# A residual block on one Trainium2 core: eight VectorE adds of the input transform given to accumulating transfers, with new engine orders

## The chip, the cores and the metric

The kernel runs on one core of one Trainium2 chip. The metric is the device time of one execution in microseconds, lower is better. A core has TensorE (PE: matmuls; PEld is its weight load), VectorE (DVE), ScalarE (ACT), GpSimd (POOL), the DMA-issuing SyncE (SP) and 16 DMA engines. In the profile, L642 is line 642 of the kernel.

## The reference

One residual block of a diffusion network. The input x is 2 images of 512 channels and 64 x 64 pixels, in bf16.

```python
def gn(z, gamma, beta): ...          # group norm over 4 groups of 128 channels, eps 1e-5
def conv3(z, w): ...                 # 3 x 3 convolution, 512 to 512 channels, padding 1
h = conv3(silu(gn(x, g1, be1)), w1)
h = h + (silu(t_emb) @ w_emb).reshape(B, C, 1, 1)
h = conv3(silu(gn(h, g2, be2)), w2)
return x + h
```

## The kernel before

**Tiling.** Layer 0 is the first convolution, layer 1 the second. Each goes over 4 chunks: 2 images (b) of 2 halves (ch) with 32 rows each; chunk n is 2 * b + ch, so the third and fourth chunk are the second image. A chunk has 4 groups, one for each tile of 128 output channels (ot); each group sums over 4 tiles of 128 input channels (ct). Each convolution is done in a transformed form: along the rows of the image four output rows come from six transformed input rows (pos 0 to 5), and for some positions a smaller transform is nested along the columns. So every chunk needs a transformed input V, every output tile a transformed weight U, and each group's results are put together again behind the matmuls.

**What each engine does.** TensorE runs direct matmuls of 512 columns (L935, into `acc` and `mid`) and nested ones of 256 columns (L943, into `nst`). PSUM holds three double banks (`ps_two`: `nst`, `mid` and small helpers) and two single ones (`ps_acc`). In layer 0 the first two groups are flat (no nesting), the third and fourth chunk nest four positions.

- `produce_V` makes V for one chunk, in steps for each ct. `activate` loads the rows into one of two buffers `ak`, and applies normalization and SiLU on ScalarE (L628) into the padded part of the buffer (65 columns a row). `transform` then makes `diff = -4 * same + below` in two instructions, a scaled copy of 128x2080 and an add on VectorE (L642); `diff` lies where the loaded rows lay. Then come an in-place subtraction of rows of the padded part (L649), a scaled copy of 520 elements, and the additions that write V (L669 reads `diff`, L679 reads `diff` and the rows), and `columns` for the nested planes (L559, L564).
- `prep_U` makes U for a weight tile: four scaled copies (1536 or 768 elements), adds on VectorE (L422) and in part an accumulating transfer issued on GpSimd (L433); `nest_U` adds the nested matrices (L395).
- Behind the matmuls of a group: evacuation of PSUM into `rm` (1024 elements) by `evac_nested` or `evac_mid`, column additions on VectorE (L988, L989, L990), row additions and three scaled copies of 512 (L1002 to L1009), evacuation of two single banks into `ring` (`close_group`), then an accumulating transfer z onto y issued on GpSimd (L1070), the store, and sums for the second norm on ScalarE (L796).

**Scaled copies and FLIP.** Every scaled copy and evacuation goes through one helper. `times` has VectorE as its default, `evac` ScalarE; a string of 406 digits, taken one by one in program order, flips the engine where it has a 1. On ScalarE such a copy shows as L308 ACTIVATE, on VectorE as L309 TENSOR_SCALAR.

**Order.** A planner (`_Background`) spreads the work of `produce_V`, `prep_U` and `nest_U` over the groups in program order. At the end `in_order` overrides this: the table `ORDER` gives for each engine the sequence of its instructions by their number in program order, written out by hand as ranges, and each instruction is made to follow the one before it. So each engine's queue is exactly its table.

The lines in which VectorE's first sum stands:

```python
D_BY_DMA = lambda layer, n, ct: False
...
if D_BY_DMA(layer, 2 * b + ch, ct):                 # in activate
    times(diff, same, -4.0)
    nc.gpsimd.dma_start(out=diff, in_=below, accum_op=ALU.add, max_dma_last_dim=CR * WP)
...
if not D_BY_DMA(layer, 2 * b + ch, ct):             # in transform
    times(diff, same, -4.0)
    nc.vector.tensor_tensor(out=diff, in0=diff, in1=below, op=ALU.add)
```

CR * WP is 32 * 65 = 2080 and HW // 2 is 2048.

Of the kernel before, what the change touches and what calls it, by code (L numbers as in the profile page):

```python
# [10 lines left out]
ALU = mybir.AluOpType  # L11
# [53 lines left out]
0-31 90-122 32-43 123 44-56 124 156 125 157-162 126 163-172 127-136 173-181 137-153 182-187 154-155 57-73 188 74-79  # L65
189-252 80-89 254 286 255 287-317 256-258 253 320-335 259-277 336-351 278-285 318 358 370-385 359-360 352-353
386-401 354-355 319 356-357 364-369 408-410 420-423 402-403 424-435 361-362 414 404-407 415-419 363 411-413 458 461
436-451 459 452-453 460 462-463 454 464-465 455 466 470-485 467 456-457 468-469 486-501 511-512 508 502-503 509
514-519 504-507 510 513 520-525 544-549 526-533 550 534-536 551 537 552-553 538-542 592-593 543 554-559 568 560-565
580 566-567 569-570 581-583 571-572 594 573-575 595 576 584-585 596-600 586-589 601-608 624-625 590-591 626-634 609  # L70
635-638 577-579 639-644 610-621 645 648 622-623 646-647 649-654 673 661 674 655-659 675 660 662-670 689 705-716 671
717-721 672 722-725 676 726-728 677-678 690-701 737 702-703 738 704 679-680 749-750 681-687 751-752 688 753-760
739-744 729-730 745 761 731-736 762 746 763 777 747-748 778-779 793-815 780-786 825-826 787-789 816 827 790-792 837
828 764-776 829-835 838 836 839-848 817 849 865 850-851 818 852 819-822 866-867 853-857 823 868-869 824 870-871 858
872 859 873 860-864 874-879 881 880 882-903 905-907 904 913 908 914-915 925 909 916 926 910-912 937-938 917 927-928
939-940 918 929-931 919 953 941-945 954 920 932 946 921 947-949 922 955-957 950 969 923 951-952 924 958 933-936
959-966 970-974 967-968 975 1001 976-978 1002-1004 1013 979-992 1005 1014-1015 993 1006 1016-1018 994 1025-1026
1019-1022 1027 1023 1028-1030 1007 1024 1031-1032 995-1000 1033-1036 1008-1009 1037-1038 1010-1011 1039-1040 1012
1041 1057-1058 1042 1059-1060 1043 1061 1044-1048 1062-1063 1049-1050 1064-1065 1051-1054 1066-1075 1055-1056
1076-1087 1109 1088 1097 1089 1110-1111 1090-1091 1112-1120 1125-1132 1092-1093 1141 1133 1142 1134-1136 1094 1137  # L80
1095 1138-1140 1098-1099 1121-1124 1100 1096 1101-1108 1143-1147 1157-1172 1148-1156 1173-1181 1185-1193 1182-1183
1194 1184 1195-1209 1213 1210-1212 1214-1242 1245-1260 1243 1261-1262 1285-1291 1263-1264 1244 1265-1267 1301-1302
1268-1284 1303-1315 1317-1319 1292 1316 1320-1327 1293-1295 1328-1332 1296-1300 1349-1353 1361-1362 1354-1357
1333-1348 1363 1358-1359 1373-1381 1360 1364 1382-1386 1365-1367 1387-1389 1405 1390-1394 1368-1371 1395-1404 1372
1406-1429 1437 1430-1431 1438-1441 1432-1436 1442-1443 1450-1451 1444-1448 1452-1459 1462-1463 1460-1461 1464
1478-1493 1449 1494-1495 1465-1477 1496-1502 1526-1528 1538 1529-1531 1539-1541 1510-1518 1542 1503-1509 1543
1519-1525 1532-1537 1544-1551 1566-1581 1552-1565 1582-1614 1626-1627 1615-1619 1628-1631 1638-1639 1620-1624 1632
1625 1633-1636 1654-1661 1637 1662-1670 1640-1653 1671-1701 1726-1730 1702 1731 1703 1732-1737 1704-1705 1714-1716
1706-1710 1717-1719 1711-1713 1720-1725 1742-1744 1738-1741 1745-1746 1758 1747-1749 1759-1760 1750-1757 1761-1770
1774-1777 1790-1798 1778-1785 1799 1802 1814 1771 1786-1787 1772-1773 1800 1803-1804 1788-1789 1805 1815-1816  # L90
1806-1809 1801 1810-1813 1830 1846 1831 1847 1832 1848-1853 1833 1854-1861 1834-1835 1862-1864 1817-1829 1865-1869
1836-1845 1894-1909 1870-1874 1882 1910-1912 1883-1891 1913 1926-1928 1875-1881 1929-1930 1914-1918 1892 1931-1940
1893 1919 1941-1951 1920-1925 1952-1961 1974-1985 1962-1963 1990-1992 1964 1993 1965-1967 2006-2007 1968-1969 2008
1994 2009-2012 1995-2000 1970-1971 2001-2005 2013-2015 1972-1973 2016-2025 2030-2033 2026-2028 2034-2035 1986 2036
2042-2045 2037 2046 2029 2047 1987 2048 1988-1989 2049 2038-2039 2050-2053 2040-2041 2054 2070-2071 2086 2055-2056
2087-2088 2057-2059 2089 2060-2064 2090 2072 2091 2065-2069 2073-2075 2092 2076-2077 2093 2078-2085 2094-2101 2110
2102 2111-2113 2103-2105 2123 2114 2124-2131 2115 2106-2109 2116-2117 2135-2136 2132 2137-2140 2151 2141-2145 2133
2118 2146 2167 2152 2119 2147-2149 2153 2120 2150 2134 2154-2156 2121-2122 2157-2159 2168-2171 2160-2164 2172
2165-2166 2173-2178 2183-2198 2179-2181 2199 2182 2200-2201 2211 2202-2205 2212 2223 2206-2208 2224-2226 2239-2241
2227-2231 2255-2258 2232 2259 2213 2260-2263 2242-2243 2214-2217 2209-2210 2218-2219 2244 2220-2222 2245 2233-2236  # L100
2246 2237-2238 2247-2252 2264 2253-2254 2265-2270 2287-2289 2271-2286 2290-2294 2299-2300 2311-2321 2327 2322
2328-2339 2301 2323-2326 2340-2342 2302-2303 2343-2344 2304 2295 2345 2296-2298 2305-2307 2346 2308-2310 2347-2354
2359-2372 2355-2356 2373 2357-2358 2374 2399-2414 2375-2377 2387-2396 2378-2380 2415-2421 2381-2382 2422-2423
2383-2384 2424-2426 2385-2386 2427-2430 2397-2398 2431-2446 2463-2464 2447-2462 2465-2471 2475 2487 2476 2488-2489
2477-2481 2503-2504 2482-2486 2505 2519-2521 2472-2474 2506-2509 2522-2525 2490-2502 2526 2510-2516 2527-2528
2517-2518 2529-2534 2551-2556 2535-2550 2557-2563 2575-2583 2591 2584 2564-2566 2607 2585-2587 2592 2588-2590 2608
2593 2567 2594 2568-2574 2609-2611 2595-2606 2612-2620 2623-2625 2639 2626-2628 2621-2622 2629 2640-2641 2663
2630-2631 2664-2665 2632-2635 2651 2636-2638 2666-2667 2652 2642 2668 2643-2644 2669 2653-2654 2670 2645-2646
2671-2672 2647-2648 2673-2677 2655 2678-2679 2656-2659 2680 2660 2681 2695 2682 2661 2683-2685 2662 2686-2690
2696-2701 2691-2694 2702-2704 2649-2650 2705-2726 2751-2764 2727-2728 2739 2765-2766 2740 2729-2733 2741-2742  # L110
2734-2737 2743 2767-2769 2744 2738 2770-2772 2783-2784 2773-2777 2745 2778 2746 2779-2780 2747-2748 2785-2786
# [76 lines left out]
def kernel(  # L188
# [13 lines left out]
    nc = tc.nc  # L202
# [5 lines left out]
    HW = H * W  # L208
    WP = W + 1
# [5 lines left out]
    CR = TH * TR  # L215
# [7 lines left out]
    D_BY_DMA = lambda layer, n, ct: False  # L223
# [372 lines left out]
    def produce_V(layer, b, ch, resident=None, V=None):  # L596
# [13 lines left out]
        def activate(ct):  # L610
            at, same, below, diff = views(ct)
# [616 lines left out]
```

## Time and profile before

| | |
|---|---|
| time, median of 3 runs | 460.19 us (459.31 to 460.53) |
| the profiled execution | 459.56 us, of which the span from the first to the last instruction is 457.5 us |
| TensorE busy | 444.0 us (97%) |
| VectorE busy | 431.4 us (94%) |
| ScalarE busy | 386.8 us (85%) |
| GpSimd busy | 75.6 us (17%) |
| mean granted TensorE clock | 0.995 |

Busy is the share of time in which an engine has an instruction in it; neighbouring instructions can overlap a little, and a busy TensorE is not TensorE at its peak. A line of a group reads: line, engine, operation, output<-input, shapes, count | busy us, mean ns of one | idle us before them, and who ended it. In the table of waits a line reads: engine, its output, line <- releasing engine, output, line: us in total, times, longest. In the table by stage each line is a stretch: length, then busy us and instructions of PE, PEld, DVE, ACT and POOL, the granted clock, the DMA engines' share and GB/s. In a timeline a line reads: start us, us from the first start to the last end, engine, line, operation, count [idle before <- releaser].

### The profile page before, as it was taken

The numbers are of one execution on the slowest core, as the hardware profiler recorded it, in microseconds if no ns is written. First come the engines' busy times: TensorE is split into PE (matmuls) and PEld (weight loads), VectorE is DVE, ScalarE is ACT, GpSimd is POOL, SyncE is SP. The second block draws the span as 40 slices with busy tenths as digits, with TensorE's granted clock in tenths as the row PEclk, the third lists the DMA queues.
The fourth block names the chain that finished last, engine by engine and source line by source line (L and its number), as shares of the span: only waits on it lengthen the run. The fifth ranks groups of instructions, "written<-read, shape, count | busy, mean of one in ns | idle before, by whom it ended". The sixth has DMA issues, their size and how long they took to land.

```text
span 457.5 us, 8442 instructions
## 1 busy us (share of the span) xinstructions
PE 444.0 (97%) x3238; PEld 288.3 (63%) x3238; DVE 431.4 (94%) x828; ACT 386.8 (85%) x423; POOL 75.6 (17%) x119
## 2 busy tenths in 40 slices
PE   8989999999999999997999999999999999999996
PEld 7944454556555667665556655557666666668874
DVE  2999999999999999999999999998999989999796
ACT  5899999979998798789999999647878697969761
POOL 1222301020000001210121211113221221222110
PEclk9999999999999999999899999999999999999999
DMA  8999765543846462447879895466957768637654
GB/s 311 353 388 243 153 169 150 161 128 104 192 128 159 101 179 64 122 141 210 221 171 262 219 208 117 115 139 163 214 142 185 181 162 210 138 92 150 128 159 165
DMA packets 25011, 80.05 MB, mean 175 GB/s; under 512 B 2827, under 2 KB 6027, under 8 KB 24587
## 3 DMA queue, kind: packets, MB, share of 16 engines
q0 software_dynamic: 10080, 34.87, 37.4%
q1 hardware_dynamic: 14832, 44.64, 28.8%
q8 instruction: 25, 0.41, 0.3%
q14 instruction: 15, 0.12, 0.1%
q10 hardware_dynamic: 59, 0.01, 0.0%
HBM read 42.54 MB, written 16.78 MB: 130 GB/s over the span
## 4 chain that ended last, share of the span: by engine, by line
PE 66%; DVE 18%; ACT 6%; issue 5%; DMA 2%; POOL 1%; SPq 0%; DVEq 0%; ACTq 0%; POOLq 0%
PE nst L943 26%; PE acc L935 23%; PE mid L935 13%; DVE V L679 2%; DVE ak L642 2%; DMA xbuf<-in_x_dram 2%; PE acc L1038 2%; DVE V L559 1%; ACT ak L628 1%; ACT rm L308 1%; ACT ring L796 1%; PE half L935 1%; DVE ak L649 1%; DVE V L564 1%; DVE V L669 1%
## 5 line engine op out<-in xcount | busy, mean ns | idle before, releaser
L943 PE MATMUL nst<-V,U 128*128 128x256 f16 x1600 | 209.5, 272 | 3.6 <-DVE rm L309 2.4
L943 PEld LDWEIGHTS <-U 128*128 128x128 f16 x1600 | 153.8, 97 | 54.8 <-issue 4.7
L935 PE MATMUL acc<-V,R 128*128 128x512 f16 x696 | 182.7, 385 | 2.0 <-DVE V L669 0.9
L935 PEld LDWEIGHTS <-R 128*128 128x128 bf16 x744 | 71.7, 97 | 64.9 <-issue 3.3
L308 ACT ACTIVATE rm<-nst 128x1024 f16<-128x1024 f32 x98 | 97.7, 1023 | 10.2 <-PE nst L943 4.7
L935 PE MATMUL mid<-V,U 128*128 128x512 f16 x336 | 85.1, 384 | 0.7 <-DVE U L422 0.7
L796 ACT ACTIVATE ring<-ring 128x2048 f16<-128x2048 f16 x32 | 61.3, 1914 | 1.6 <-ACT ak L628 0.6
L628 ACT ACTIVATE ak<-ak,nb_all,sc_all 128x2112 f16<-128x2112 f16 (+1 forms) x28 | 60.1, 2153 | 2.3 <-DVE nb_all L527 2.3
L935 PEld LDWEIGHTS <-U 128*128 128x128 f16 x336 | 32.4, 97 | 36.1 <-DVE U L422 1.4
L308 ACT ACTIVATE ring<-ring 128x512 f16<-128x512 f16 x58 | 34.9, 626 | 22.7 <-DVE ring L1002 15.9
L1070 POOL DMA_DIRECT2D ring<-ring x28 | 26.5, 946 | 143.3 <-ACT ring L308 122.1
L308 ACT ACTIVATE ak<-ak 128x520 f16<-128x520 f16 (+1 forms) x34 | 38.2, 1141 | 3.0 <-DVE ak L649 2.8
L642 DVE TENSOR_TENSOR ak<-ak 128x2080 f16<-128x2080 f16 x32 | 39.9, 1248 | 0.1
L679 DVE TENSOR_TENSOR V<-ak 128x1040 f16<-128x1040 f16 x54 | 39.2, 726 | 0.7 <-ACT ak L308 0.5
L990 DVE TENSOR_TENSOR rm<-tu,rm 128x1024 f16<-128x1024 f16 x50 | 34.8, 695 | 1.0 <-ACT rm L308 0.8
L564 DVE TENSOR_TENSOR V<-V 128x512 f16<-128x512 f16 (+1 forms) x62 | 35.3, 577 | 0.0
L559 DVE TENSOR_TENSOR V<-V 128x1024 f16<-128x1024 f16 (+1 forms) x31 | 30.8, 995 | 0.7 <-PE acc L935 0.7
L308 ACT ACTIVATE ring<-acc 128x512 f16<-128x512 f32 x52 | 29.6, 596 | 1.8 <-DVE ring L309 0.8
L422 DVE TENSOR_TENSOR U<-U,g1t 128x1536 f16<-128x1536 f16 x32 | 30.9, 972 | 0.0
L989 DVE TENSOR_TENSOR tu<-rm 128x512 f16<-128x512 f16 x50 | 21.4, 428 | 2.7 <-ACT rm L308 2.5
L649 DVE TENSOR_TENSOR ak<-ak 128x1040 f16<-128x1040 f16 x32 | 23.0, 718 | 0.1
L669 DVE TENSOR_TENSOR V<-ak 128x1040 f16<-128x1040 f16 x32 | 22.9, 715 | 0.0
(132 smaller groups left out, 452.4 us busy)
## 6 DMA issues: line engine op xcount, KB each, us to landing
ring<-ring POOLq DMA_DIRECT2D x28, 512.0 KB, 4.6
ak<-h_scr SPq DMA_DIRECT2D x16, 528.0 KB, 3.9
h_scr<-ring SPq DMA_DIRECT2D x16, 512.0 KB, 3.7
ring<-in_x_dram POOLq DMA_DIRECT2D x14, 512.0 KB, 5.6
out_dram<-ring POOLq DMA_DIRECT2D x14, 512.0 KB, 4.7
ak<-in_x_dram SPq DMA_DIRECT2D x12, 528.0 KB, 4.3
R<-in_w_dram SPq DMA_DIRECT2D x16, 384.0 KB, 4.7
U<-U POOLq DMA_DIRECT2D x14, 384.0 KB, 5.7
```

The source lines that it names most:

```text
L308: return nc.scalar.activation(out=o, in_=i, func=ACT.Copy, scale=f)
L422: nc.vector.tensor_tensor(out=o, in0=i0, in1=i1, op=op)
L559: nc.vector.tensor_tensor(out=lo2.rearrange("p c q (t w) -> p (q t) c w", w=HALF), in0=plane_pair(0, HALF + 2), in1=plane_pair(1, HALF), o ...
L564: nc.vector.tensor_tensor(out=hi2[:, c].rearrange("p q (t w) -> p (q t) w", w=HALF), in0=i0, in1=i1, op=op)
L628: nc.scalar.activation(out=at[:, lo - r0:hi - r0, 1:W + 1], in_=sap, func=ACT.Silu, bias=nb_all[:, layer, b, ct:ct + 1], scale=sc_all[:, l ...
L642: nc.vector.tensor_tensor(out=diff, in0=diff, in1=below, op=ALU.add)
L649: nc.vector.tensor_tensor(out=rows(1, 2), in0=rows(1, 2), in1=rows(3, 2), op=ALU.subtract)
L679: nc.vector.tensor_tensor(out=o, in0=in0, in1=in1, op=op)
L796: behind(nc.scalar.activation(out=junk, in_=y, func=func, scale=scale, accum_out=acc), inst)
L935: nc.tensor.matmul(out, lhsT=w_direct(pos, ct, kx), rhs=rhs, start=first, stop=last)
L943: nc.tensor.matmul(accs["nst", (pos - 1) // 2][bank][:, q, :, plane, :], lhsT=lhsT, rhs=rhs.rearrange("p (t w) -> p t w", w=HALF), start=s ...
L990: nc.vector.tensor_tensor(out=msl[:, 1 - k:4 - k:2].rearrange("p q t w -> p q (t w)"), in0=tu[:].rearrange("p q t e w -> p q (t e w)"), in ...
```

## The change

In the third and fourth chunk of layer 0 (8 cases: 2 chunks, 4 ct) the first sum of the input transform is made in `activate`: the scaled copy, then a transfer issued on GpSimd that adds 2048 of the 2080 elements of each partition (4096 bytes), and an add of the last 32 elements on VectorE. The switch string is another (103 ones instead of 138, of 406), and so are the tables: VectorE has 855 entries instead of 824, ScalarE 354 instead of 385, GpSimd 123 instead of 115; TensorE (3231) and SyncE (103) have as many as before, in another order.

```diff
     "DVE": """
-0 4 3 2 1 14 13 5 7 6 48 8 16 9 15 10 17 11 20 12 19 18 25-26 22 27 21 28 23 29 24 30-31 46 32-33 47 49 34 52 35 53
+0 4 3 2 1 13-14 5 7 48 6 8-10 15-16 11 17 19 18 25 24 12 21 26 20 27 22 28 23 29-32 45 33 38 46 49 47 34 50 35 51 70
...
-    D_BY_DMA = lambda layer, n, ct: False
+    D_BY_DMA = lambda layer, n, ct: layer == 0 and n >= 2
...
-    FLIP = "0100100011000000000000100010010100000110100001110111001100001100110000000011000000010011100000111001000001010000011000100011100000000000100111000010001000000000100000001010100010100000010001000000111011110000000001001101101000000000001110010000100101110011000011011111000001010000000111100000100111010000001111100000001100000100111110000001111100001100111000000111110000001110000110000111000000001010000111"
+    FLIP = "1000110010101011000000000000000010001011100000000111001100000001101100000000000000001100000000000001010000110000000100000001000000000000000000000000110000001000000000000000000000000100000001000000111011100000000000100100010100001001011001010000111000011011000010011101000001000000000001100001000111111000000110000000010000000100111010000001100100000100111000000101110000001100000100000101000000001110000111"
...
             if D_BY_DMA(layer, 2 * b + ch, ct):
                 times(diff, same, -4.0)
-                nc.gpsimd.dma_start(out=diff, in_=below, accum_op=ALU.add, max_dma_last_dim=CR * WP)
+                nc.gpsimd.dma_start(out=diff[:, 0:HW // 2], in_=below[:, 0:HW // 2], accum_op=ALU.add,
+                                    max_dma_last_dim=HW // 2)
+                nc.vector.tensor_tensor(out=diff[:, HW // 2:], in0=diff[:, HW // 2:], in1=below[:, HW // 2:], op=ALU.add)
```

In program order the calls of the string that concern the first chunk of layer 0 are 8, 10, 12 and 14 for the four scaled copies of 2080 elements, and 9, 11, 13 and 15 for those of 520.

The start of TensorE's table, before and after. Entries 352 to 369, 402 to 419, 452 to 469 and 502 to 519 are the first group's matmuls for ct 0 to 3, entries 520 to 591 the second group's; 320 to 351, 370 to 401, 420 to 451 and 470 to 501 are column sums of the second image:

```diff
-... 411-413 458 461 436-451 459 452-453 460 462-463 454 464-465 455 466 470-485 467 456-457 468-469 486-501 511-512 508 502-503 509 514-519 504-507 510 513 520-525 544-549 526-533 ...
+... 414-419 436-451 461-462 458-460 470-485 463 452-454 464-465 455 466-467 456-457 468-469 511 508 512 486-501 509-510 520-528 513 502-505 514 506-507 515-517 529-531 518-519 532-542 ...
```

More of the change, by code (lines that the diff above doesn't have):

```diff
@@ L70 @@
[L70 to L84, printed above, removed]
@@ new lines @@
+1351 1373-1378 1352 1379-1385 1361-1362 1386-1388 1353-1354 1363 1355-1360 1389 1364-1366 1390-1404 1367-1372
+1405-1414 1421-1428 1437 1429-1436 1438-1439 1415 1440 1416-1420 1441-1443 1450-1452 1444 1453-1454 1445 1455
+1446-1449 1456-1464 1478 1465-1470 1479-1484 1471-1476 1485-1486 1477 1526 1494 1487-1491 1495 1492-1493 1496-1507
+1527 1508-1523 1538 1528-1529 1524-1525 1530-1532 1539-1546 1533-1535 1550 1566-1569 1551-1555 1570-1571 1582
+1572-1576 1583 1547-1549 1584 1536-1537 1577 1585-1595 1578-1581 1596-1597 1556-1565 1614-1620 1626 1598-1613
@@ L171 @@
+85 79 89-100 102 101""",
 }
```

181 lines of the change are left out of this document (95 added, 86 removed).

## The prediction

> **What bounds the kernel now.** First the page: busy shares and the granted clock by slice.
>
> ```profile
> PE 444.0 (97%) x3238; PEld 288.3 (63%) x3238; DVE 431.4 (94%) x828; ACT 386.8 (85%) x423; POOL 75.6 (17%) x119
> ...
> PEclk9999999999999999999899999999999999999999
> ```
>
> TensorE is the bound and its matmuls are not touched, so the change can win only where TensorE now waits or is slowed. Next, who TensorE waited for (total us, times, longest):
>
> ```profile
> PE nst L943 <- DVE rm L309: 2.4, 1, 2.4
> ...
> PE nst L943 <- ACT rm L308: 1.2, 3, 0.8
> PE acc L935 <- DVE V L669: 0.9, 1, 0.9
> PE acc L935 <- DVE V L662: 0.8, 1, 0.8
> ...
> PE mid L935 <- DVE U L422: 0.7, 1, 0.7
> ```
>
> Two of these lie in the start (0.9 at 33 us, 0.7 at 46 us). The larger ones lie in the last chunk of layer 0. The table by stage (us; busy of PE, PEld, DVE, ACT, POOL; clock; DMA) shows it:
>
> ```profile
> 150.00:200.00 50.00, 50.00 (x360) 34.38 (x358) 48.67 (x101) 41.24 (x46) 6.52 (x8) 1.00 0.46 128
> 200.00:210.00 10.00, 9.16 (x60) 5.54 (x58) 9.97 (x20) 10.00 (x12) 1.22 (x3) 1.00 0.57 135
> 210.00:220.00 10.00, 7.63 (x58) 5.93 (x57) 10.00 (x20) 9.49 (x14) 1.96 (x3) 0.88 0.66 206
> 220.00:232.00 12.00, 11.18 (x75) 7.09 (x73) 12.00 (x22) 11.38 (x12) 0.81 (x2) 0.96 0.93 238
> 232.00:300.00 68.00, 68.00 (x413) 39.70 (x412) 67.69 (x124) 63.52 (x72) 12.65 (x18) 1.00 0.75 175
> ```
>
> From 200 to 232 us VectorE and ScalarE are both full and TensorE is idle for 0.84 + 2.37 + 0.82 = 4.0 us. From 150 to 207 us the chain that ended last runs through VectorE almost alone. After the 2.37 us the clock is down as well. The timeline shows twelve `acc` matmuls at 2.82 us before and 3.58 us behind it:
>
> ```profile
> 206.30 2.82 PE L935 MATMUL acc<-V,R 128*128 128x512 f16 x12
> ...
> 215.47 1.23 DVE L309 TENSOR_SCALAR rm<-nst 128x1024 f16<-128x1024 f32 x1
> ...
> 219.39 3.58 PE L935 MATMUL acc<-V,R 128*128 128x512 f16 x12
> ```
>
> The granted clock gives the price: 10 x 0.12 + 12 x 0.04 = 1.7 us. With some 0.7 us of shorter gaps the last chunk of layer 0 loses 4.0 + 1.7 + 0.7 = 6.4 us. That is what can be won. The Trainium skill (TensorE: Matmul & The Clock Gate, Part 1) puts the drop to half clock behind an idle window of about 3.4 us. By that rule 2.37 us would cost no clock and 4.7 us could be won; the trace shows the drop, and I take 6.4.
>
> **The eight adds.** In chunks three and four of layer 0 the full add (L642, 128x2080) leaves VectorE; these eight ran at 102.7 to 179.8 us, all ahead of the loss.
>
> ```profile
> L642 DVE TENSOR_TENSOR ak<-ak 128x2080 f16<-128x2080 f16 x32 | 39.9, 1248 | 0.1
> L308 ACT ACTIVATE ak<-ak 128x2080 f16<-128x2080 f16 x13 | 25.3, 1943 | 0.2
> L309 DVE TENSOR_SCALAR ak<-ak 128x2080 f16<-128x2080 f16 x19 | 13.4, 705 | 1.2 <-ACT ak L628 1.2
> L1070 POOL DMA_DIRECT2D ring<-ring x28 | 26.5, 946 | 143.3 <-ACT ring L308 122.1
> ```
>
> Removed: 8 x 1.248 = 10.0 us. Added: eight 32-column tails. No row has that shape. Adds of 512, 1040 and 2080 columns take 428, 718 and 1248 ns, about 0.53 ns a column and 167 ns fixed, so 0.18 us; the 4- and 8-column adds (160 to 200 ns) agree. Eight are 1.4 us. Bounds 0.07 us (the V memset) and 0.43 us (512 columns). VectorE: -8.6 us.
>
> **The switch string.** Ones fall from 138 to 103 of 406, and the tables go from 824 to 855 entries on VectorE and from 385 to 354 on ScalarE: 31 scaled copies net move to VectorE. Walking the string along the calls (the eight -4.0 copies are now called one step earlier) gives, net: 18 row copies of 512 (0.303 us on VectorE, 0.626 on ScalarE), 8 of 520 (0.307, 0.645), 6 weight copies of 1536 (0.565, 1.487), one 2080, one row copy, minus one 768; two evacuations of 1024 go the other way (1.227, 1.023). VectorE: 5.5 + 2.5 + 3.4 + 0.7 + 0.3 - 0.4 - 2.5 = +9.5 us. ScalarE: -25.0 us. So VectorE as a whole stays where it was (-8.6 + 9.5 = +0.9), and ScalarE is relieved. One of the two evacuations is the 1.23 us row at 215.47 that ended the longest wait.
>
> **The transfers.** GpSimd gets 8 more issues (about 0.9 us each, 7 us of an engine at 17%). The DMA engines are 46 to 53% busy at 100 to 200 us, and the nearest transfer (`ring<-ring`, 512 KB, same accumulate) lands 4.6 us after its issue starts, 4.0 to 7.5 over all accumulates. Who waits is the subtraction at L649 or L669 on VectorE, and behind it VectorE's whole queue. In the new table 5.55 to 10.5 us of VectorE rows stand between each copy and the first such reader. Row durations add to 503 us against 431.4 busy, since neighbours overlap, so the cover lasts 0.857 of that: 4.8, 4.9 and 5.1 us for the three tightest (third, first and fifth transfer), 6.4 to 9.0 for the rest. I take the cost as nothing; if transfers take the 7.5 us of the slowest, the tight ones wait 2 to 3 us each. On GpSimd each transfer also stands ahead of a z-add (L1070) that, before, waited on GpSimd for ScalarE; if a copy comes late, that add, its store and the sums behind it come late too. Copies move up with their SiLUs, so I take nothing.
>
> What lengthens an issue is seen at 50 us:
>
> ```profile
> 50.13 2.07 POOL L1070 DMA_DIRECT2D ring<-ring  x1 [6.62 <-DVE V L559]
> ...
> 54.22 0.86 POOL L433 DMA_DIRECT2D U<-U  x1 [1.13 <-ACT U L308]
> ```
>
> The 2.07 us issue lay beside 1.7 us of VectorE scaled copies (L309) and the 1.44 us one at 176 us beside 0.7 us; most beside adds alone took 0.86 to 0.9. The Trainium skill (SBUF — State Buffer, Who interferes with whom) has the reason: scaled copies in two-port mode lock GpSimd's descriptor writing out, adds do not. The trace agrees, though some issues beside 0.7 to 0.9 us of copies stayed at 0.87. This speaks against the change, which puts more such copies on VectorE: up to 1.2 us on a landing (2.07 - 0.86). It belongs to the late-landing rival below.
>
> **The start.** The new string also moves work in the first 50 us, where no transfer is added. Of the four -4.0 copies of chunk one, three that ran on VectorE (0.705) go to ScalarE (1.943), and the tables put 9.0 us more ScalarE work ahead of its first PSUM evacuation (42.9 against 33.9 us of rows) and 8 us more VectorE work ahead of the last piece of V (45.1 against 37.2). ScalarE is full from 20 us on, so that evacuation moves from 42.2 to about 51; the last piece of V, finished at 40.6, moves 8 x 0.857, to about 47. TensorE meanwhile gets nine matmuls of the second group early. In the trace it had done 84 wide matmuls when its last wait of the start ended at 46.85; by the new tables it has done 72 at 47, since the last channel tile needs those pieces. Twelve at 0.2214 us (2.21 us for ten in the chain) are +2.7 us. Bounds: 0, if the next wait (for U, at 46) was the real limit, and +9, if the whole ScalarE delay shows.
>
> **The last chunk of layer 0.** All evacuations there are now on ScalarE, with 4 to 10 us less ScalarE work ahead of each, and TensorE comes 2.7 us later, which gives the others time. TensorE alone would then end at +2.7 - 6.4 = -3.7 us. VectorE: rows ahead of its additions at L990 fall by 0.6 to 5.7 us between 197 and 235 us, 4.3 at 235 and at 294, 2.3 at 307 us; times 0.857, VectorE allows -3.7 down to -2.0 us. What is late next is therefore VectorE. I take the middle, **-2.9 us**. Behind 310 us VectorE has idle time (2 to 3 us in each 20), and I take nothing there.
>
> The profiled execution took 459.56 us (span 457.5 and 2.1 around it); the median of the runs is 460.19, 0.63 more. Forecast: 459.56 - 2.9 = 456.7 in its terms, **457.3** as a median.
>
> **Rivals.**
> - Slower, by the start. The point that decides is ScalarE's first evacuation: if TensorE has nothing to do until it is done, all 9.0 us show and the half clock comes once more (1.7 us); the 6.4 us then vanish anyway. 459.56 + 9.0 + 1.7 - 6.4 = 463.9, median 464.5. For it: ScalarE at 10.0 of 10 us from 20 to 30. Against: a third pair of PSUM banks lets group two begin. 0.22.
> - Slower, by late landings. With landings at 7.5 us, or issues stretched by the copies beside them, VectorE stands 1.2 us at each of the eight and its 9.6 us are spent again: no gain at the boundary, +2.7 from the start: 462.3, median 462.9. Against: `ring<-ring` of the same size landed in 4.4 to 4.9 us at 69 to 154 us. 0.12.
> - It does not do what it says. VectorE's total is unchanged, so the loss shrinks only by what the start adds: 459.6, median 460.2. For it: +0.9 us on VectorE. 0.16.
> - The boundary loss goes and the start costs nothing: 459.56 - 6.4 = 453.2, median 453.8. 0.12.
> - Forecast: 0.38.
>
> A measurement of this kernel can tell about 0.3%, 1.4 us, from no change. Faster: 0.38 + 0.12, less 0.02 for the forecast's weak end: 0.48. Same: 0.16 + 0.02 = 0.18. Slower: 0.22 + 0.12 = 0.34. The range goes from the best case, 453.8, to 463.5, which leaves out the far half of the start rival and a tenth at the edges. The forecast's own range is 454.5 to 459.
>
> **What would show it.** Right: no TensorE wait over 1 us and clock 1.00 between 190 and 240 us; the first evacuation near 50 us; eight GpSimd issues between 85 and 175 us landing in under 5.5 us; no VectorE wait for a DMA at L649 or L669; ScalarE busy about 362 us, VectorE about 432. Wrong: a TensorE wait of several us at 35 to 57 us, a half-clock stretch there, VectorE idle behind a transfer, or new waits in layer 1.

## Result and profile after

| | before | changed |
|---|---|---|
| time, median | 460.25 us (459.31 to 460.53) | 474.57 us (472.26 to 477.34) |
| profiled execution / its span | 459.56 / 457.5 us | 474.57 / 472.8 us |
| VectorE / ScalarE / GpSimd busy | 431.4 / 386.8 / 75.6 us | 430.4 / 367.8 / 84.2 us |

Four runs each; the ratio is 1.032 (95% interval 1.026 to 1.0375): the change costs some 14 us, where I forecast 457.3 and gave 463.5 as the upper end.

The first lines of the page of the changed kernel, busy shares and granted clock:

```profile
PE 448.2 (95%) x3238; PEld 289.4 (61%) x3238; DVE 430.4 (91%) x859; ACT 367.8 (78%) x392; POOL 84.2 (18%) x127
...
PEclk9997999999999999999999999899999999999998
```

VectorE has the work that was forecast (432) and ScalarE is relieved, but TensorE's share went down. There is a new half-clock stretch at the fourth digit (36.5 to 43.4 us). The table by stage, with the stretches of the prediction (us; busy of PE, PEld, DVE, ACT, POOL; clock; DMA share; GB/s):

```profile
150.00:200.00 50.00, 46.26 (x332) 31.58 (x329) 44.98 (x93) 39.37 (x42) 7.00 (x10) 1.00 0.66 164
200.00:210.00 10.00, 10.00 (x68) 6.41 (x67) 9.32 (x27) 8.07 (x8) 2.21 (x4) 1.00 0.40 107
210.00:220.00 10.00, 10.00 (x75) 6.94 (x73) 10.00 (x21) 9.77 (x11) 0.91 (x1) 1.00 0.73 198
220.00:232.00 12.00, 12.00 (x85) 7.88 (x83) 12.00 (x25) 11.42 (x11) 2.04 (x3) 1.00 0.72 184
232.00:300.00 68.00, 62.73 (x389) 37.29 (x387) 63.30 (x115) 58.12 (x66) 11.25 (x15) 1.00 0.75 179
```

From 200 to 232 us TensorE is full at clock 1.00: the loss that was to be won is gone. But it loses 3.7 us in the 50 us ahead of that and 5.3 us in the 68 us behind it, and VectorE, 48.67 us busy at 150 to 200 us before, now stands 5 us there. Who TensorE waited for (us in total, times, longest):

```profile
PE nst L944 <- ACT rm L307: 5.5, 6, 2.9
PE acc L936 <- ACT ring L307: 4.4, 3, 2.2
PE acc L936 <- DVE V L670: 2.0, 1, 2.0
```

Fixed stretches of time mislead when one kernel is late, so I compare at equal work. A matmul of 512 columns counts 0.221 us and one of 256 columns 0.108 us (start to start, undisturbed); with the small ones at their own spacing TensorE's matmuls add to some 434 us in every kernel, and its lateness is the time less the work done. By stretch of work, the lateness that TensorE gains, and VectorE's busy and idle time in the same stretch (all us, from the traces):

| work done | lateness, before | after | VectorE busy / idle, before | after |
|---|---|---|---|---|
| 0 to 40 | 8.7 | 14.0 | 39.1 / 8.3 | 41.3 / 11.3 |
| 40 to 200 | 2.0 | 7.2 | 159.2 / 2.7 | 155.5 / 11.6 |
| 200 to 220 | 5.3 | 1.0 | 25.4 / 0.0 | 21.1 / 0.0 |
| 220 to 300 | 0.4 | 9.9 | 78.9 / 1.6 | 83.9 / 6.0 |
| 300 to the end | 2.4 | 1.6 | 127.5 / 8.7 | 127.3 / 8.2 |
| sum | 18.8 | 33.7 | | |

One traced execution stands behind each column. In seven kernels whose engine orders agree up to 50 us the first stretch comes out up to 2 us apart, so smaller differences tell little.

So +5.3 at the start, +5.2 around the transfers, -4.3 at the boundary as hoped, +9.5 in the first part of layer 1: +14.9, with the span 15.3 longer. All that follows uses this table.

**Around the transfers.** Each moves as 256 packets of 2048 bytes, although a partition has 4096: the limit `max_dma_last_dim=HW // 2` is 2048, a row has 2048 elements, and the packets come out half a row long. An issue takes 1.21 us (a z-add 0.9), and the landing comes 5.0 to 7.2 us after the issue starts. The waits for them, GpSimd's and VectorE's, in the table of waits:

```profile
POOL ak L614 <- DMA ak<-ak: 8.5, 2, 6.0
...
DVE ak L650 <- DMA ak<-ak: 4.0, 3, 3.0
```

The transfers also hold each other up. GpSimd's timeline has the fifth, a z-add and the sixth:

```profile
145.41 1.20 POOL L635 DMA_DIRECT2D ak<-ak  x1 [12.31 <-DVE U L394]
147.83 0.92 POOL L1071 DMA_DIRECT2D ring<-ring  x1 [1.22 <-ACT ring L307]
150.77 1.21 POOL L635 DMA_DIRECT2D ak<-ak  x1 [2.01 <-DVE ee L394]
```

The scaled copy for the sixth ended at 147.43, yet its issue starts 3.3 us later, 0.31 us after the fifth has landed (145.41 + 5.05 = 150.46). The profile names VectorE as releaser, but the second, fourth and eighth transfer also start 0.32 to 0.33 us after the landing of the one before. Seven of the kernels here have halved packets: in them this is so 25 times, and none of these transfers is issued while another is under way. In the four kernels with whole packets that happens ten times. Why it is so is not shown.

The sixth transfer (issued at 150.77, landed 7.2 us later) shows what a late landing does. VectorE, then ScalarE, then TensorE, each in its timeline:

```profile
158.04 0.71 DVE L650 TENSOR_TENSOR ak<-ak 128x1040 f16<-128x1040 f16 x1 [3.03 <-DMA ak<-ak]
...
159.50 0.68 DVE L1003 TENSOR_TENSOR ring<-rm 128x1024 f16<-128x1024 f16 x1
```

```profile
160.27 1.94 ACT L307 ACTIVATE rm<-nst 128x1024 f16<-128x1024 f32 x2 [1.14 <-DVE ring L1003]
```

```profile
161.35 2.35 PE L944 MATMUL nst<-V,U 128*128 128x256 f16 x20 [2.89 <-ACT rm L307]
```

VectorE stands 3.03 us at the subtraction; the row addition queued behind it (L1003) comes late, so `rm` comes free late, ScalarE's evacuation into it too, and TensorE waits 2.89 us. The last releaser is ScalarE; the transfer stands two engines behind it.

**First part of layer 1.** Here VectorE waits for a z-add (issued at 288.90, landed 8.9 us later), ScalarE for VectorE, TensorE for ScalarE:

```profile
297.80 0.69 DVE L1005 TENSOR_TENSOR ring<-rm 128x1024 f16<-128x1024 f16 x1 [2.75 <-DMA ring<-ring]
```

```profile
298.53 0.63 ACT L307 ACTIVATE ring<-ring 128x512 f16<-128x512 f16 x1 [6.37 <-DVE ring L1005]
299.06 2.14 ACT L627 ACTIVATE ak<-ak,nb_all,sc_all 128x2112 f16<-128x2112 f16 x1
301.10 1.06 ACT L307 ACTIVATE ring<-acc 128x512 f16<-128x512 f32 x2
```

```profile
301.73 1.78 PE L936 MATMUL acc<-V,R 128*128 128x512 f16 x6 [2.25 <-ACT ring L307]
```

### The profile page after: what moved, and what is told of

Same layout as the page of the kernel before. It is cut to its first block, busy times and chain, and to the rows that moved or that the text cites. A ratio compares the mean times of both kernels' runs of the same rounds, so it can differ in the third digit from the quotient of the medians.

```text
span 472.8 us, 8477 instructions
## 1 busy us (share of the span) xinstructions
PE 448.2 (95%) x3238; PEld 289.4 (61%) x3238; DVE 430.4 (91%) x859; ACT 367.8 (78%) x392; POOL 84.2 (18%) x127
## 3 DMA queue, kind: packets, MB, share of 16 engines
q0 software_dynamic: 12256, 39.06, 41.3%
## 5 line engine op out<-in xcount | busy, mean ns | idle before, releaser
L307 ACT ACTIVATE rm<-nst 128x1024 f16<-128x1024 f32 x100 | 100.3, 1022 | 25.0 <-PE nst L944 11.3
L1071 POOL DMA_DIRECT2D ring<-ring x28 | 25.1, 896 | 131.8 <-ACT ring L307 121.6
L307 ACT ACTIVATE ak<-ak 128x520 f16<-128x520 f16 (+1 forms) x25 | 31.6, 1263 | 11.5 <-DVE ak L650 8.7
L680 DVE TENSOR_TENSOR V<-ak 128x1040 f16<-128x1040 f16 x54 | 38.4, 711 | 0.7 <-ACT ak L307 0.7
L307 ACT ACTIVATE ring<-ring 128x512 f16<-128x512 f16 x40 | 24.0, 622 | 18.1 <-DVE ring L1003 10.2
L563 DVE TENSOR_TENSOR V<-V 128x512 f16<-128x512 f16 (+1 forms) x62 | 34.0, 560 | 0.0
L421 DVE TENSOR_TENSOR U<-U,g1t 128x1536 f16<-128x1536 f16 x32 | 30.1, 949 | 0.5 <-DMA U<-U 0.5
L643 DVE TENSOR_TENSOR ak<-ak 128x2080 f16<-128x2080 f16 x24 | 29.7, 1237 | 0.2
L650 DVE TENSOR_TENSOR ak<-ak 128x1040 f16<-128x1040 f16 x32 | 22.6, 705 | 4.0 <-DMA ak<-ak 4.0
L1005 DVE TENSOR_TENSOR ring<-rm 128x1024 f16<-128x1024 f16 x28 | 19.2, 685 | 5.1 <-DMA ring<-ring 3.4
```

What stands on the lines that cost most here:

```text
L307: return nc.scalar.activation(out=o, in_=i, func=ACT.Copy, scale=f)
L421: nc.vector.tensor_tensor(out=o, in0=i0, in1=i1, op=op)
L563: nc.vector.tensor_tensor(out=hi2[:, c].rearrange("p q (t w) -> p (q t) w", w=HALF), in0=i0, in1=i1, op=op)
L680: nc.vector.tensor_tensor(out=o, in0=in0, in1=in1, op=op)
L1071: add_z = lambda: nc.gpsimd.dma_start(out=flat(yst), in_=ring[:, NY + turn % NZ], accum_op=ALU.add)
```

## Experiments

Each kernel ran beside runs of the kernel before on the same chip (medians 459.4 to 460.3 us); intervals are of the ratio to it. "Stretch" is one of the five above, named by its work.

### What the transfers cost

**Whole packets.** The changed kernel without the packet limit.

```diff
-    nc.gpsimd.dma_start(out=diff[:, 0:HW // 2], ..., accum_op=ALU.add, max_dma_last_dim=HW // 2)
+    nc.gpsimd.dma_start(out=diff[:, 0:HW // 2], ..., accum_op=ALU.add)
```

> The changed kernel with the size limit of the eight transfers left out. In its trace each transfer runs as 256 packets of 2048 bytes with issues of 1.2 us and landings of 5.0 to 7.2 us; here I expect 128 packets of 4096 bytes, issues near 0.9 us and landings near 4.5 us, as the z-adds have. If the transfers cause the loss (theory A: late landings hold VectorE and, in GpSimd's queue, the z-adds), the time falls from 474.6 to about 465 to 469 us. If the tables cause it (theory B: the new orders put work late at the start and in the first chunk of layer 1), it stays within 2 us of 474.6.

472.12 us, ratio 1.028 (1.025 to 1.030). There are 128 packets of 4096 bytes, and most issues take 0.86 to 0.92 us, as expected. The landings I had expected near 4.5 us, but they take 4.6 to 8.3 us (median 6.0, and 5.9 with halved packets). What changes is the start: the fourth, sixth and eighth transfer no longer stand behind the landing of the one before (the sixth is issued 0.9 us after its copy, not 3.3), VectorE's waits at the subtraction fall from 4.0 to 1.0 us, and stretch 40 to 200 loses 3.9 us instead of 7.2. In total time the halved packets cost some 2.5 us by the medians, with intervals that overlap.

**New tables, sums on VectorE again, no transfers.**

```diff
-D_BY_DMA = lambda layer, n, ct: layer == 0 and n >= 2     # GpSimd's table loses its 8 new entries
+D_BY_DMA = lambda layer, n, ct: False                     # the full add stands where the 32-column one stood
```

> The tables and the switch string of the changed kernel, but the eight sums are full adds on VectorE again (each in the place of its 32-column tail) and GpSimd has no transfer for them. Theory A: VectorE gets 8.6 us of work back and nothing lands late; 460 to 466 us. Theory B: the losses at the start (+5 us) and in layer 1 (+9 us) remain, 472 to 478 us.

475.97 us, ratio 1.035 (1.031 to 1.038), as theory B expected: the new string and tables are slow by themselves. Given those, transfers with whole packets win 3.9 us; the 1.4 us of the halved ones lie within the scatter of the runs.

**New tables, no transfers and no sums.** As the last, with the sums cut to 32 columns (the other 2048 columns are left out): transfers that cost nothing.

```diff
-    nc.vector.tensor_tensor(out=diff, in0=diff, in1=below, op=ALU.add)
+    lo_ = HW // 2 if layer == 0 and 2 * b + ch >= 2 else 0
+    nc.vector.tensor_tensor(out=diff[:, lo_:], in0=diff[:, lo_:], in1=below[:, lo_:], op=ALU.add)
```

> The changed kernel (its string and tables) with no transfers at all: the eight sums are cut to the last 32 columns, the first 2048 are left out. It is the changed kernel with transfers that cost nothing and are never waited for. Theory (VectorE paces the kernel: time is its busy time plus its idle time, and of its 10.0 us idle at 100 to 200 us some 6 to 7 stand behind transfers and the z-adds queued behind them): 467 to 469; the remaining 7 to 9 us over the kernel before are start and layer 1. Rival (VectorE's idle time there only reflects that something else is late, such as ScalarE or TensorE): 472 or more.

469.10 us, ratio 1.020 (1.016 to 1.023), at the theory's upper end. Stretch 40 to 200 falls from 7.2 to 2.9 us: the transfers, their issues and their landings cost 4.3 us of the 5.2 there, and 5.5 us of the total time. The 9.7 us over the kernel before (459.44 beside it) come from string and tables alone.

**Old tables, no sums.** The same cut in the kernel before.

> The kernel before, its tables and string unchanged, with the eight sums of the third and fourth chunk of layer 0 cut to the last 32 columns and nothing in their place (the first 2048 columns of each sum are left out): what transfers that cost nothing would bring. Theory (VectorE, without idle time from 50 to 310 us, is what TensorE waits for at 200 to 232 us): VectorE's 8.6 us go, the loss of 6.4 us there goes with them, 453 to 455.5. Rival (ScalarE, as full in that stretch, is late next): 457.5 to 460.

459.59 us against 459.44, ratio 1.000 (0.9987 to 1.0012). This is the run that decides: my theory's 453 to 455.5 did not come. With eight sums for nothing the old order gains nothing. The table by stage of this kernel:

```profile
100.00:150.00 50.00, 50.00 (x318) 28.57 (x317) 44.82 (x82) 47.53 (x49) 3.43 (x8) 1.00 0.52 143
150.00:200.00 50.00, 50.00 (x362) 34.50 (x360) 46.10 (x100) 41.65 (x48) 6.00 (x8) 1.00 0.45 128
200.00:232.00 32.00, 28.79 (x197) 19.39 (x195) 31.98 (x60) 31.33 (x34) 4.00 (x7) 0.95 0.74 197
```

VectorE's work at 100 to 200 us fell from 97.9 to 90.9 us, and TensorE is 50.00 of 50 as before: the freed time became idle time, while at 200 to 232 VectorE is as full as ever.

**Old tables with transfers,** whole packets and halved ones (readers moved back by 0.6 to 4 us).

```diff
 DVE, each of the 8 cases
-sum L643; subtraction L650; ...
+32-column sum; (other entries for 0.6 to 4 us); subtraction L650; ...
```

> The tables and the string of before, with the eight transfers in packets of 4096 bytes: each add becomes its 32-column tail in the same place, the transfer is queued on GpSimd at the end of its copy, and the readers of one channel tile (L650 to the columns) move back in VectorE's table by 0.6 to 4 us so that about 5 us lie between copy and first reader. Theory B (only the new tables are at fault; the transfers do what the prediction said): VectorE has 8.6 us less ahead of the loss at 200 to 232 us, which shrinks from 6.4 to 0 to 2 us; 455 to 458 us. Theory A (transfers hold VectorE and GpSimd's queue whatever the tables): 461 to 466 us.

> As the run before it, but with the change's own size limit, which gives 256 packets of 2048 bytes a transfer. If the packets cost by their landing (about 1.4 us later) and their issue (0.35 us longer), 1 to 3 us more than with whole packets; if only the tables matter, the same within 1 us.

With whole packets 480.45 us, ratio 1.045 (1.043 to 1.048), far above what either theory had; with halved ones 485.55, 1.057 (1.052 to 1.061), 5.1 us more where I expected at most 3. From the waits with whole packets:

```profile
DVE ak L650 <- DMA ak<-ak: 10.8, 7, 3.1
```

```profile
POOL ak L615 <- DMA ak<-ak: 18.4, 4, 5.7
```

From the end of each copy to its first reader VectorE here has 3.2 to 6.3 us of cover, waits taken out, where the changed kernel has 5.9 to 9.7, and it stands at seven of eight subtractions. GpSimd's memset of the next buffer waits for the same landing, and the z-adds queued behind it wait too. So the transfers need an order that gives them more cover; the new tables give it, and are themselves the larger cost. Other orders were not tried.

### Where in time

**The start of before** (engine and place of all that starts before 50 us in the kernel before), rest new; **layer 1 of before** (all behind 245 us), rest new; **only the middle new** (50 to 245 us, whole packets).

```diff
-ORDER, FLIP of the changed kernel
+ORDER, FLIP: [before: < 50 us] + [changed: rest]
+ORDER, FLIP: [changed: < 245 us] + [before: rest]
+ORDER, FLIP: [before: < 50 us] + [changed: 50 to 245 us] + [before: rest]
```

> Every instruction that the kernel before starts in its first 50 us keeps the engine and the place of before; all the rest goes by the new tables, with the transfers. Theory B: the start loses 7.4 instead of 12.4 us, and about 5 us come off: 469 to 470 us, first evacuation at 42 instead of 52 us. Theory A: the losses behind the start fill up again, within 2 us of 474.6.

> The new tables, string and transfers up to 245 us of the changed kernel's trace (the end of layer 0); what starts later goes by the engines and the order of before. Theory B: the TensorE waits at 250 to 306 us (9.5 us with the half clock, against 0.5 before) go, 465 to 467 us. Theory A, in the form that the transfers leave layer 0's tail late and layer 1 only pays for it: the waits stay, 472 to 476 us.

> Three parts: what the kernel before starts in its first 50 us and what the changed kernel starts after 245 us go by the engines and the order of before; only the stretch between, with the eight transfers (in packets of 4096 bytes), goes by the new tables. If the three table effects add up (start -0.9, layer 1 -4.7, packets -2.5 from 474.6, as measured one by one), 466 to 467 us. If the new tables of the middle alone cost nothing (theory A's opposite), 460 us; if the three measured effects overlap, 469 us.

A seam is the place where one order passes into the other.

- Start of before: 473.64 us, ratio 1.030 (1.027 to 1.032), not 469 to 470. The start is back at 9.4 us of lateness, but the seam loses 3.9 us at work 40 to 60, so the pieces hang together.
- Layer 1 of before: 469.87 us, 1.022 (1.018 to 1.026), between the two theories. Stretch 220 to 300 falls from 9.9 to 4.5 us, of which 4.1 lie at the seam (a wait of 2.6 us and half clock behind it); behind the seam the old order loses almost nothing, so layer 1's loss belongs to its new order.
- Only the middle new: 466.05 us, 1.013 (1.011 to 1.016), the sum of the three effects, as expected.

**Only the middle new, without sums or transfers** (2048 columns of each sum left out, as above).

> As the kernel with the new order from 50 to 245 us only (466.05), but with no transfers: the eight sums are cut to the last 32 columns, the first 2048 left out. Theory: of VectorE's 8.6 us idle at 100 to 200 us there, 5 to 6 stand behind transfers: 460 to 461.5. Rival (the seams at 55, 64 and 247 us and the new order itself hold it): 464 to 466.

465.02 us, ratio 1.012 (1.009 to 1.015). The rival was right: without transfers it is only one microsecond less. The seams lose 3.7 us at work 40 to 60 and 3.2 at 220 to 230, most of what this kernel loses.

### Mends that did nothing

**GpSimd's order of before behind 245 us**, all else as changed.

```diff
 Pool, behind 245 us
-order of the changed kernel
+order of the kernel before
```

> The changed kernel, but behind 245 us GpSimd's queue has the order of before: in the first chunk of layer 1 two z-adds then stand ahead of a weight transfer that they stood behind. If GpSimd's queue makes the TensorE waits at 260 to 306 us (z-adds issued 11 to 12 us later than before), 2 to 5 us come off, 470 to 472 us; if VectorE's and ScalarE's tables make them, 474 us within 1.5 us.

472.95 us, ratio 1.029 (1.027 to 1.032). The changed kernel ran at 472.26 to 477.34, so this tells little.

**Three copies of the start back on VectorE**, and **three evacuations of layer 1 moved ahead on ScalarE**, and both with whole packets.

```diff
 start: -4.0 copy of chunk one, ct 1 to 3
-Activation, ahead of the sums
+DVE, right before the sum
 layer 1, Activation
+ring<-acc (283.96)
 L797 (282.07)
+ring<-acc (301.10)
 L307 ring<-ring (298.53)
+ring<-acc (301.58)
 L627 (299.06)
```

> The changed kernel with three scaled copies of 128x2080 (the -4.0 copies of the first chunk of layer 0 for ct 1 to 3) on VectorE again, each right before its add; all else as in the changed kernel. In the changed kernel they stand on ScalarE at 21.9, 31.5 and 38.3 us, 3 x 1.94 = 5.8 us ahead of the first evacuation (52.3 us), and TensorE loses 12.4 us in the first 50 us instead of 7.4. Theory (ScalarE's queue of the start is what is late): the first evacuation comes 4 to 6 us earlier, the loss before 50 us falls to 8.5 to 10, time 470 to 472.5. Rival (the start hangs on the statistics, whose small VectorE operations stand behind weight copies, and on VectorE's later V pieces, which get 3 x 0.7 us more ahead of them): the waits at 34 and 36 us stay, time 474 to 476.

> The changed kernel with three evacuations of 512 elements (ring<-acc) moved ahead on ScalarE in layer 1: the one at 283.96 us ahead of the second sum that starts at 282.07, the first of the two at 301.10 ahead of the row copy that stood 6.4 us until 298.53, the second of them ahead of the SiLU at 299.06. Theory (PSUM evacuations stand in ScalarE's order behind instructions that wait for a z transfer): TensorE's waits of 1.9 us at 282 and 2.3 us at 299 and the half clock at 303 to 306 (1.7 us) vanish, time 468 to 470.5. Rival (ring places, or VectorE, which stands behind the same transfer at 297.8, are late next): the waits come back within 10 us, time 473 to 475.

> The changed kernel with three things at once: transfers in packets of 4096 bytes, the three copies of the start back on VectorE, the three evacuations of layer 1 moved ahead. If the losses stand side by side, it is 474.6 less 2.5 (packets, measured) less what the other two give alone, 461 to 466. If each mend only lets the next late thing show, it stays above 468.

Three copies back: 476.50 us, ratio 1.035 (1.034 to 1.037). Three evacuations ahead: 474.61, 1.032 (1.029 to 1.036). Both with whole packets: 473.05, 1.027 (1.025 to 1.029). My theory of late evacuations fell. With the evacuations ahead, TensorE's waits at 282 and 299 us went and one of 2.2 us came at 286 to 288: stretch 220 to 300 loses 9.5 us as against 9.9, and VectorE is idle 5.9 us as against 6.0. With the copies back, in the stretch up to 40 us of work ScalarE's busy time fell from 44.9 to 39.5 us, VectorE's rose from 41.3 to 43.4, and the lateness rose from 14.0 to 15.9: it did not go with ScalarE's work, and it rose with VectorE's. Taking away the last releaser gained nothing while VectorE behind it stayed late.

### What the boundary loss of the kernel before is

Four kernels made from the kernel before, with nothing of the change: the late evacuation moved ahead; the small statistics entries moved ahead; VectorE relieved inside 200 to 232 us (first 2048 columns of four sums left out); ScalarE relieved there (1792 of 2048 elements left out of twelve sums for the second norm).

```diff
 DVE
 L1004 (211.39)
+L1002 (214.05)
 ...
+rm<-nst (215.47)
 L564 (212.46)
 Activation
+rm<-nst (215.96)
 L308 ring<-ring (212.88)
```

```diff
 DVE
 L321 (189.97)
+L330, L331, L332
 ...
 L990 (192.10)
+L340, L341, L526, L342, L527
```

```diff
+    lo_ = HW // 2 if layer == 1 and 2 * b + ch == 0 else 0          # in the sum of transform
```

```diff
+    y, junk = y[:, 0:256], junk[:, 0:256]                             # in sum_up, last six pairs
```

> The kernel before, with nothing of the change, and three entries of its tables moved in the last chunk of layer 0: on VectorE the row addition L1002 of 214.05 us comes right behind L1004 of 211.39, and the evacuation of 215.47 (rm<-nst, 1.23 us), which ended the 2.37 us wait of TensorE, comes ahead of five entries of V and rows (212.46 to 215.27); on ScalarE the evacuation of 215.96 comes ahead of two row copies and a SiLU (212.88 to 215.44). Theory (in-order queues: an evacuation that stands behind work that nobody waits for costs TensorE its wait and the half clock behind it): the wait of 2.37 us and the 1.7 us of half clock go, 456 to 458.5. Rival (V's pieces, now 1.2 us later on VectorE, are late next): 459.5 to 461.

> The kernel before, with nothing of the change, and eight small entries of VectorE's table (statistics of the first image for the second norm, L330 to L332, L340 to L342, L526, L527, 0.16 us each) moved ahead: the first three right behind L321 (189.97 us), the other five right behind the addition L990 of 192.10. In the kernel before they lie scattered up to 195.94, and ScalarE's first SiLU of layer 1 stood 2.32 us for the last of them. Freeing VectorE of the eight sums ahead of this point left the loss at 200 to 232 us as it was (459.59), and VectorE ran its entries from 196 us on at the same times. Theory (the last chunk of layer 0 is set by what starts with these statistics, not by VectorE's work ahead of them): the SiLU starts some 2 us earlier, TensorE's wait of 2.37 us at 216 shrinks, the half clock behind it goes wholly or in part, 456.5 to 458.7. Rival (the evacuations' and rows' work in that stretch is set by TensorE itself and by the full queues, the SiLU only fills ScalarE's gap): 459.3 to 460.3.

> The kernel before, tables and string unchanged, with the four sums (L642) of the first chunk of layer 1 cut to the last 32 columns (the first 2048 columns of each are left out). They run at 201 to 232 us, inside the stretch in which VectorE and ScalarE are both full and TensorE loses 6.4 us: some 3.2 us of VectorE less up to 221 us. Theory (the loss at 200 to 232 us is set by VectorE's own work inside that stretch): TensorE's loss there falls by 2.5 to 4 us and some half clock goes with it, 455.5 to 458. Rival (ScalarE, as full there): 459 to 460.5.

> The kernel before, tables and string unchanged, with the last twelve sums for the second norm on ScalarE (L796, from 198 us on) taken over 256 instead of 2048 elements (1792 elements of each are left out): some 9 us of ScalarE less between 198 and 230 us, VectorE's entries as they were. Theory (VectorE's work inside the stretch sets the loss): 458.5 to 460, TensorE still waits for the evacuation on VectorE at 216 us. Rival (ScalarE's work inside the stretch sets it): the loss falls by 3 us or more, 454.5 to 457.

| | time | ratio (interval) | lateness 200 to 220 | VectorE busy there | ScalarE busy there |
|---|---|---|---|---|---|
| before | 459.4 to 460.3 | 1 | 5.3 | 25.4 | 24.5 |
| evacuation ahead | 461.34 | 1.003 (1.002 to 1.004) | 7.7 | 26.7 | 26.1 |
| statistics ahead | 459.69 | 1.000 (0.998 to 1.001) | 4.5 | 24.6 | 24.3 |
| VectorE relieved | 458.76 | 0.997 (0.995 to 0.998) | 3.9 | 22.9 | 23.9 |
| ScalarE relieved | 459.16 | 0.997 (0.996 to 0.999) | 5.0 | 25.0 | 20.6 |

The evacuation that ended the 2.37 us wait, moved ahead, made it worse than either forecast: the wait fell to 0.5 us, and new ones of 1.8 and 2.9 us came at 217 and 230 us. With the statistics ahead the time stayed, as the rival had it. ScalarE relieved, from its table by stage and TensorE's timeline:

```profile
200.00:232.00 32.00, 28.91 (x198) 19.58 (x196) 31.97 (x60) 23.75 (x33) 3.99 (x7) 0.95 0.74 196
```

```profile
216.47 3.52 PE L947 MATMUL nst<-V,U 128*128 128x256 f16 x16 [2.56 <-ACT rm L308]
```

ScalarE gave up 7 us from 200 to 232 us and TensorE waits as long as before, now "for ScalarE", so ScalarE's amount of work does not make this wait. With VectorE relieved, its table by stage reads:

```profile
200.00:232.00 32.00, 27.80 (x203) 19.23 (x201) 30.71 (x64) 32.00 (x38) 4.15 (x8) 1.00 0.74 199
```

TensorE is idle there for 4.2 us against 4.0 before; what went is the half clock (0.95 to 1.00, 32 x 0.05 = 1.6 us). VectorE's work in the stretch 200 to 220 fell by 2.5 us, and 1.0 us of the time is now idle. The two relieved kernels ran at the same 0.997 of the kernel before, so their times cannot tell VectorE from ScalarE; only the lateness in the stretch does (3.9 and 5.0 against 5.3). So the cause of the boundary loss is not settled. Runs exclude the eight sums and the one late evacuation, and the wait that stayed speaks against ScalarE's amount of work. That VectorE has 25.4 us of work there against 20 of matmuls, and that the new tables cut the work and the loss by 4.3 us each, fits VectorE as the pace, but relieving it alone brought 1.4 us. What holds the rest stays open. No kernel that computes the whole block was faster than the kernel before.

## Why the prediction was wrong, by its steps

- **VectorE's total: right.** The tails took 172 ns each (0.18 forecast), VectorE 430.4 us (432 forecast). ScalarE's busy time fell by 19.0 us, not 25.0: the forecast added row durations, which in the traces fell by 26.3, while busy time counts an overlap once.
- **"Rows ahead of its additions at L990 fall ..., VectorE allows -3.7 down to -2.0": the step that failed.** The rows were nearly right: up to 300 us of work VectorE had 302.6 us busy before and 301.8 after. But the step took VectorE's time to go as its rows do, so that its idle time stayed as it was, and that rose from 12.6 to 28.9 us up to the same point: +3.0 at the start, +8.9 around the transfers, +4.4 in layer 1, together 16.3 against 15.7 us more lateness there. That the two sums agree is bookkeeping, since time is busy time plus idle time and busy time did not change; it shows which term of the forecast was missing, and what made VectorE idle is told by the waits and runs below. It also took time saved at 103 to 180 us as time to spend at 200 to 232. At 40 to 200 us of work VectorE had 159.2 us of work for 160 of matmuls, so TensorE set the pace there, and the old order without sums turned the savings into idle time (from 2.7 to 9.6 us).
- **The boundary: the right loss, not for the reason given.** It fell from 5.3 to between 1.0 and 1.4 us in every kernel with the new middle, with or without transfers or sums. VectorE's work there fell from 25.4 to 21.1 us, in part since work was put off: additions for U (L421, 0.97 us) fall from four to two there and rise from twelve to fourteen in the stretch behind it.
- **Layer 1: not in the sum.** I took nothing behind 310 us and let VectorE's rows speak for 232 to 310, where the table by stage shown in the prediction had VectorE at 67.69 of 68. Work 220 to 300 got 83.9 us of VectorE for 80 us of matmuls, and 4.4 us more idle time, behind z-adds and row sums among others: the largest term, +9.5 us. That the new order of layer 1 is the cause is shown (the old order there leaves 4.5 us, 4.1 of them at a seam; leaving out the transfers leaves 8.4); how it splits between put-off work and waits is read from the table, not tried.
- **"Transfers: I take the cost as nothing": wrong by 4.3 us.** They landed in 5.0 to 7.2 us, not 4.6, and the step counted the landing from the end of the copy, with nothing between copy and issue, where 0.4 to 3.3 us lay. So the long wait, 3.0 of the 4.0 us at L650, came at the sixth transfer, which the step had among the safe ones: 7.6 us from copy to reader, 3.3 of them gone before the issue. Of the third, first and fifth, called the tightest, only the third waited (0.7 us). What was queued behind these waits came late. The late-landing rival had the mechanism and gave 9.6 us. Of its two causes, long landings showed; copies that stretch an issue did not, as most issues fell from 1.21 to 0.86 to 0.92 us with the packet size alone.
- **The start: the direction right, the size not.** The first evacuation came at 51.4 us (51 forecast) and the last piece of V at 49.2 (47), yet TensorE lost 5.3 us more, not 2.7. The mis-sized term is the count of matmuls: at 47 us TensorE had done 62 wide ones, not the 72 that I took (84 before). It waited 1.95 us until 38.27 for a piece of V of ct 2, which came at 37.53 instead of 33.41. In VectorE's timeline twelve weight copies now stand between the pieces for ct 1 and ct 2, where three did (the string and the order moved them there). The last of them, the sum and the piece:

```profile
34.74 1.09 DVE L308 TENSOR_SCALAR U<-R 128x768 f16<-128x768 bf16 x3
35.75 1.23 DVE L643 TENSOR_TENSOR ak<-ak 128x2080 f16<-128x2080 f16 x1
...
37.53 0.69 DVE L670 TENSOR_TENSOR V<-ak 128x1040 f16<-128x1040 f16 x1
```

  From 36 to 44 us the granted clock was 0.57, 8 x 0.43 = 3.4 us. It fell at 36.53, just as this wait began, and a wait of 1.40 us for a load of x had ended at 35.77. I had priced the half clock only in the rival. The weight copies as the cause are read, not tried; that ScalarE's three copies are not the cause was tried.
- **The rivals.** "Slower, by the start" gave 464.5 and let the boundary's gain pay for it. No case held the losses at the start, around the transfers and in layer 1 at once, so no case reached 474.

## What to carry to other kernels

Compare an engine's work with the bottleneck's by stretches of equal work, not over the whole kernel: work saved where the bottleneck sets the pace turned into idle time here, and work put off into a full stretch seems to have been paid there (read from the table, not tried). Count the new waits of an in-order queue with its work, since what is queued behind a late transfer is late on other engines too. Before asking whether a transfer can hide, time the kernel with its work left out: here that one run showed that the best case, in the old order, is no gain.

## What the runs showed of the hardware

- A limit of 2048 on the last dimension, with rows of 2048 elements or 4096 bytes, gave packets of 2048 bytes: 190 ns each, 256 in a transfer, 1.21 us an issue. Without it packets had 4096 bytes and most issues took 0.86 to 0.92 us. With the limit no such transfer was issued before the one ahead of it had landed (25 issues came 0.31 to 0.33 us behind that landing); without it ten were.
- In the changed kernel one z-add of layer 1 landed 8.9 us after its issue; in the kernel before they took 4.4 to 4.9 us at 69 to 154 us, and 4.4 to 7.5 from 243 us on. Its packets began 3.4 us after the issue, beside a load of `ak`, against 1.4 to 1.5 us for those at 69 to 154 us.
- Waits of 2.37 us (before) and 2.36 us (old order without sums) were followed by half clock at 0.88 and 0.86 in the ten microseconds; one of 2.48 us at the same place (statistics ahead) by none, 1.00. The Trainium skill (TensorE: Matmul & The Clock Gate, Part 1) puts the drop behind about 3.4 us of idle; it came at less here, and not by the length of this wait alone.
- By the clock records of the 20 traces the drops go with where a wait lies. In each trace all changes of the granted clock are whole multiples of 3.413 us apart. The wait of 2.37 us (214.38 to 216.75) lay inside one such step, 214.13 to 217.54, and the clock fell at its end. Of the 2.48 us (214.39 to 216.87) the step from 214.85 to 218.27 held 2.02, and it did not fall; nor did it behind the changed kernel's 2.89 us, which an edge cut into 0.95 and 1.94. Between 50 and 450 us all 20 steps behind which the clock fell held 2.01 us or more without a matmul, and the longest idle time behind which it did not was 2.02. So these traces put the border near 2.0 us within one step, and the 1.7 us of half clock at the boundary hang in part on where the steps fall, which differs from trace to trace.
